# One attention pipeline for the first two blocks, weights queued later, the later casts moved from GpSimd to ScalarE, and the query permutation moved from the gate multiply to the exponential

## The chip, the cores and the metric

The kernel runs on one core of one Trainium2 chip. The metric is the device time of one execution in microseconds (us). Most executions of one kernel agree closely, but some run some per cent longer at a lower mean clock of TensorE. The runs therefore carry a state, "fast" or "slow".

In the text PE is TensorE, DVE is VectorE, ACT is ScalarE, POOL is GpSimd, and SP is the engine that issues most DMAs. "Clock" is the share of full speed that the throttle granted PE.

## The reference, cut to what matters

```python
# q, k, v: (4, 8, 768, 64); mem_k, mem_v: (4, 8, 8, 64)
for c in range(nc):                       # chunks of 32 queries
    k_ctx = k[:, :, l_start:r_end]        # 16 keys to the left, 8 to the right
    k_full = concatenate([mem_k, k_ctx]); v_full = concatenate([mem_v, v_ctx])
    a = softmax(q_c @ k_full.T / 8)
    out[:, :, c_start:c_end] = a @ v_full
x = out.transpose(0, 2, 1, 3).reshape(3072, 512)
return (relu(x @ w_gate) * (x @ w_val)) @ w_out     # FFN, 512 -> 1536 -> 512
```

The 3072 tokens are eight blocks of 384. Each block has four attention steps of 96 queries against 120 keys and 8 memory keys, then 12 FFN pieces (one for each 128 of the 1536 hidden columns) and three output products. An FFN piece is four matmuls with `w_gate` and four with `w_val`.

## The kernel before

The parts that the change and the argument touch, with cuts marked `...`. `dv`, `pl` and `act.copy` (`ac`) are copies on DVE, POOL and ACT. `x` is the output of the attention and `xT` its transpose; to "turn" a tile is to transpose it. `keep(n)` issues n matmuls whose results are never used, `outp` is one output product, and `u` counts the FFN pieces and products of a block. Keys and queries are loaded with three consecutive tokens to a partition, so after the transpose the queries of a step lie in the order "remainder by 3 first" (`t c`). The natural order is `c t`.

```python
def cast3(eng, c, n, a0=0, na=HP):        # fp32 -> f16, keys or queries of block n
    ...
def cast_v(eng, n):                       # values; memory rows by a second cast on POOL
    eng(vb_t[n % 2][:, :, :, 0:D], vraw[:, n % 2])
    ...
    pl(vb_t[n % 2][0:NMEM, :, :, 0:D], m4)
def turn_k(n): ...                        # transposing DMA on SP; turn_q(n) likewise
def diag(n): ...                          # DVE: transposed queries into a block-diagonal tile
def bands(n, eng): ...                    # copies of the transposed keys into four bands

class Step:
    def scores(self): ...                 # PE
    def soft(self):                       # ACT; the queries stay in the order t c
        ...
        act.activation(e.rearrange("p (h b) c -> p b h c" if self.early else "p (b h) c -> p b h c", b=2),
                       PS[:, 0:2, 0:384].rearrange("p b (h c) -> p b h c", h=4), ACT.Exp, scale=SCALE)
    def mask(self): ...                   # DVE: e = e * mask, both in SBUF
    def values(self): ...                 # PE
    def norm(self): ...                   # DVE: x_big
    def turn_dma(self): ...               # xT by a transposing DMA; turn_pe by PE and a copy

def dff(n, m, c0=0, c1=MB):               # an FFN piece
    ...                                   # PE, then ACT relu, then PE
    o, i0, i1 = gvT[n][:, m, c0:c1], vl_ps, g_relu[:, 0:w]
    if n not in EARLY:                    # blocks 2 to 7: the permutation is undone here
        o = o.rearrange("p (j c t) -> p j t c", t=R3, c=PP)
        i0, i1 = (z.rearrange("p (j t c) -> p j t c", t=R3, c=PP) for z in (i0, i1))
    dve.tensor_tensor(out=o, in0=i0, in1=i1, op=ALU.mult)

# between the FFN of blocks 0, 1 and the rest
cast3(dv, "k", 2)
...
turn_k(2)
cast3(dv, "q", 2)
turn_q(2)
...
outp(0, 0)
outp(0, 1)
cast_v(pl, 2)
diag(2)
bands(2, dv)
outp(0, 2)
...                                       # attention of block 2 among the products of block 1

for n in range(2, NBLK):                  # FFN of block n, attention of block n + 1, casts of n + 2
    for u in range(NDC + NT):
        ...
                if u == (10 if n == 2 else 7):
                    cast3(pl, "k", n + 2)
                    ...
                    cast3(pl, "q", n + 2)
                if u == vu[3]:
                    turn_k(n + 2)
                    turn_q(n + 2)
                if u == vu[3]:
                    cast_v(pl, n + 2)
```

The softmax here doesn't subtract the row's maximum and nothing guards it: scores larger than these inputs give would overflow.

## Time and profile before

Three runs gave 285.18, 288.53 and 282.09 us (288.53 is 2.3% above the fastest, so it counts as slow). The profiled run was a slow one (291.95 us, span 290.2, clock 0.952), so its stages are somewhat longer than those of a fast run.

The first cut is at block 1's first FFN piece, the others are where the output products of a block begin. This is the busy time by stretch. The columns are the stretch and its length, the busy time of PE, PEld (weight loads), DVE, ACT and POOL with the count of instructions, the PE clock, the DMA share and GB/s.

```profile
0.00:48.40 48.40, 38.42 (x297) 20.73 (x298) 23.07 (x60) 22.24 (x37) 36.75 (x77) 0.95 1.00 199
48.40:77.10 28.70, 28.70 (x161) 16.49 (x161) 10.60 (x19) 9.80 (x20) 4.45 (x5) 0.90 0.37 91
77.10:136.50 59.40, 43.96 (x305) 25.73 (x304) 28.79 (x57) 16.79 (x34) 10.38 (x7) 0.89 0.65 146
136.50:255.40 118.90, 107.96 (x732) 60.67 (x730) 69.31 (x108) 42.74 (x77) 42.12 (x43) 0.99 0.60 135
255.40:290.20 34.80, 31.27 (x172) 16.30 (x168) 11.24 (x16) 9.21 (x18) 0.00 (x0) 0.99 0.14 49
```

| stage | what runs in it |
|---|---|
| 0 to 48.4 ("front") | attention of blocks 0 and 1, four FFN pieces |
| 48.4 to 77.1 | the other 20 FFN pieces of blocks 0 and 1; PE never idle, but at clock 0.90 |
| 77.1 to 136.5 ("middle") | six output products, attention of blocks 2 and 3, FFN of block 2 |
| 136.5 to 255.4 ("four blocks") | products of block n, FFN of n + 1, attention of n + 2; four times |
| 255.4 to 290.2 ("tail") | what is left, with no attention |

The middle loses most: PE is busy 43.96 of 59.40 us there, and runs at clock 0.89 besides. The timeline shows why (start, duration, engine, line, operation; in brackets the engine's idle time just before it and what ended it).

```profile
77.83 0.95 DVE L169 CAST kn<-kraw 128x1536 f16<-128x1536 f32 x1
...
85.41 1.12 DVE L195 COPY qd<-qT 64x1536 f16<-64x1536 f16 x2 [5.44 <-DMA qT<-qn]
...
88.39 0.82 PE L242 MATMUL PS<-qd,kb 128*128 128x192 f16 x4 [3.38 <-DVE kb L221]
...
97.78 1.88 POOL L179 CAST vb<-memv 8x2048 f16<-8x2048 f32 x1
...
98.08 1.99 DVE L257 TENSOR_TENSOR ex<-ex,mask_int_t 128x768 f16<-128x768 f16 x1 [3.88 <-ACT ex L250]
...
100.13 0.43 PE L261 MATMUL PS<-vb,ex 128*128 128x66 f16 x8 [2.61 <-DVE ex L257]
```

Block 2's key cast starts at 77.83, after the last FFN piece. PE gets the bands at 88.39, 10.6 us later, having waited 3.38 us. At 98.08 a mask multiply beside a POOL cast takes 1.99 us, and the values product waits 2.61 us for it.

The groups of instructions (count, busy time and mean ns; then idle time before them, by releaser) give the cost of one operation.

```profile
L304 DVE TENSOR_TENSOR gvT<-PS,g_relu 128x384 f16<-128x384 f32 x92 | 67.7, 739 | 92.8 <-PE PS L298 91.3
...
L250 ACT ACTIVATE ex<-PS 128x768 f16<-128x768 f32 x32 | 26.0, 813 | 40.6 <-PE PS L242 29.3 <-DVE rinv L267 7.3 <-PE PS L238 4.0
L257 DVE TENSOR_TENSOR ex<-ex,mask_int_t 128x768 f16<-128x768 f16 x18 | 15.0, 833 | 7.5 <-ACT ex L250 7.5
```

### The profile page before, as it was taken

Reading aid. Unit: us, or ns where it says so; the run is one execution under the profiler, and the core shown is the slowest. Engines: PE = TensorE matmul, PEld = TensorE weight load, DVE = VectorE, ACT = ScalarE, POOL = GpSimd, SP = SyncE. Lnnn points to the kernel's source line nnn. Section 1 sums busy time; section 2 is a strip of 40 time slices with the busy share of each in tenths; the row PEclk is TensorE's granted clock in tenths of the full one; section 3 lists DMA queues with packets and bytes.
Section 4 is the critical chain, followed back from the end, with each engine's and each line's share of the span. In section 5 each row is a group of like instructions: output and inputs, shape, how many; then the busy total and the mean of one; then the engine's idle time right before and its main releaser. Section 6 shows DMA issues by size and latency. Waiting matters only on the chain.

```text
span 290.2 us, 4432 instructions
## 1 busy us (share of the span) xinstructions
PE 250.3 (86%) x1656; PEld 139.9 (48%) x1656; DVE 143.0 (49%) x258; ACT 100.8 (35%) x185; POOL 93.7 (32%) x131
## 2 busy tenths in 40 slices
PE   6697996999976488399977799889988999999995
PEld 2335553565523257155444455545555556645652
DVE  3418453344523316738355751875187517733630
ACT  2435564233221234134132423343334325423321
POOL 6828897022004500500454502652255140000000
PEclk9999797799997979969997999999999999999999
DMA  7998993930099519805399219971996180121002
GB/s 212 314 235 110 206 204 52 273 78 0 2 204 264 192 35 222 179 0 98 101 236 266 42 27 187 285 132 29 213 289 114 27 220 0 27 66 72 1 4 107
DMA packets 81237, 38.66 MB, mean 133 GB/s; under 512 B 53952, under 2 KB 78272, under 8 KB 81216
## 3 DMA queue, kind: packets, MB, share of 16 engines
q1 hardware_dynamic: 74208, 32.74, 48.0%
q0 software_dynamic: 5808, 4.72, 10.5%
q10 hardware_dynamic: 1200, 0.92, 1.0%
q8 instruction: 13, 0.21, 0.3%
q14 instruction: 8, 0.07, 0.1%
HBM read 29.72 MB, written 6.29 MB: 124 GB/s over the span
## 4 chain that ended last, share of the span: by engine, by line
PE 65%; DVE 19%; DMA 6%; POOL 3%; issue 2%; ACT 2%; SPq 1%; DVEq 0%; POOLq 0%; ACTq 0%
PE PS L293 18%; PE PS L298 18%; PE PS L313 16%; DVE ex L257 6%; DVE gvT L304 5%; PE PS L261 3%; PE PS L242 3%; DMA kT<-kn 3%; PE PS L356 2%; DVE x_big L270 2%; POOL kb L211 2%; DVE kb L211 2%; DMA kraw<-in_k_dram 1%; DMA qT<-qn 1%; PE PS L333 1%
## 5 line engine op out<-in xcount | busy, mean ns | idle before, releaser
L304 DVE TENSOR_TENSOR gvT<-PS,g_relu 128x384 f16<-128x384 f32 (+1 forms) x100 | 71.4, 718 | 94.8 <-PE PS L298 91.3
L293 PE MATMUL PS<-xT,w_gate_sb 128*128 128x384 f16 (+1 forms) x400 | 82.9, 332 | 1.1 <-ACT xT L280 1.1
L298 PE MATMUL PS<-xT,w_val_sb 128*128 128x384 f16 (+1 forms) x400 | 82.8, 332 | 0.0
L296 ACT ACTIVATE g_relu<-PS 128x384 f16<-128x384 f32 (+1 forms) x100 | 47.7, 477 | 60.0 <-PE PS L293 43.9
L313 PE MATMUL PS<-w_out_sb,gvT 128*128 128x512 f16 x288 | 66.5, 389 | 0.0
L298 PEld LDWEIGHTS <-w_val_sb 128*128 128x128 f16 x400 | 40.0, 101 | 26.3 <-issue 4.1
L293 PEld LDWEIGHTS <-w_gate_sb 128*128 128x128 f16 x400 | 39.7, 101 | 24.9 <-issue 4.8
L313 PEld LDWEIGHTS <-gvT 128*128 128x128 f16 x288 | 28.6, 100 | 33.6 <-issue 3.3
L250 ACT ACTIVATE ex<-PS 128x768 f16<-128x768 f32 x32 | 26.0, 813 | 40.6 <-PE PS L242 29.3
L323 ACT COPY o_sb<-PS 128x512 f32<-128x512 f32 x23 | 13.5, 587 | 56.6 <-PE PS L313 50.3
L176 POOL CAST vb<-vraw 128x2048 f16<-128x2048 f32 x6 | 11.4, 1894 | 41.7 <-DMA vraw<-in_v_dram 41.7
L261 PE MATMUL PS<-vb,ex 128*128 128x66 f16 x256 | 13.6, 195 | 11.5 <-DVE ex L257 10.0
L211 POOL COPY kb<-kT 128x480 f16<-128x480 f16 (+1 forms) x12 | 9.5, 889 | 42.2 <-DMA kT<-kn 42.2
L270 DVE TENSOR_TENSOR x_big<-PS,rinv 96x512 f16<-96x512 f32 x32 | 22.0, 686 | 1.1
L242 PE MATMUL PS<-qd,kb 128*128 128x192 f16 x96 | 13.2, 265 | 10.8 <-DVE kb L221 8.2
L169 POOL CAST kn<-kraw 128x1536 f16<-128x1536 f32 x5 | 7.3, 1469 | 44.4 <-DMA kraw<-in_k_dram 44.4
L261 PEld LDWEIGHTS <-ex 128*128 128x128 f16 x256 | 10.9, 99 | 20.7 <-ACT g_relu L296 8.4
L257 DVE TENSOR_TENSOR ex<-ex,mask_int_t 128x768 f16<-128x768 f16 x18 | 15.0, 833 | 7.5 <-ACT ex L250 7.5
L242 PEld LDWEIGHTS <-kb 128*128 128x128 f16 x96 | 7.8, 104 | 12.9 <-DVE kb L221 9.1
L169 POOL CAST qn<-qraw 128x1536 f16<-128x1536 f32 (+1 forms) x8 | 10.7, 1336 | 9.5 <-DMA qraw<-in_q_dram 9.5
L179 POOL CAST vb<-memv 8x2048 f16<-8x2048 f32 x6 | 12.1, 2023 | 0.4
L195 DVE COPY qd<-qT 64x1536 f16<-64x1536 f16 x12 | 7.7, 645 | 6.8 <-DMA qT<-qn 6.7
(106 smaller groups left out, 152.1 us busy)
## 6 DMA issues: line engine op xcount, KB each, us to landing
out_dram<-o_sb SPq DMA_DIRECT2D x23, 256.0 KB, 2.3
vraw<-in_v_dram SPq DMA_DIRECT2D x24, 240.0 KB, 7.2
kraw<-in_k_dram SPq DMA_DIRECT2D x7, 768.0 KB, 7.8
qraw<-in_q_dram SPq DMA_DIRECT2D x7, 768.0 KB, 8.7
vraw<-in_v_dram SPq DMA_DIRECT2D x2, 768.0 KB, 13.7
w_out_sb<-in_moe_w_out_dram POOLq DMA_DIRECT2D x3, 512.0 KB, 15.3
w_gate_sb<-in_moe_w_gate_dram POOLq DMA_DIRECT2D x2, 512.0 KB, 7.6
w_val_sb<-in_moe_w_val_dram POOLq DMA_DIRECT2D x2, 512.0 KB, 9.4
```

Of the source, the lines that this page charges most:

```text
L169: eng(d.rearrange("p a t (x d) -> p a x t d", x=2), raw[c][:, i, 2 * a0:2 * a0 + 2 * na].rearrange("p (a x) t d -> p a x t d", x=2))
L211: eng(dst(1, c0 + r, [[128, nj], [R3, 40]]), src(kT, TS * t + P + (r > 0), [[PP, nj], [1, 40]]))
L242: pe.matmul(o.rearrange("p (x t c) -> p x t c", x=2, t=R3), lhsT=self.kb[:, a, j, :], rhs=qd_t[i][:, a].rearrange("p x (t c) -> p x t c", ...
L250: act.activation(e.rearrange("p (h b) c -> p b h c" if self.early else "p (b h) c -> p b h c", b=2), PS[:, 0:2, 0:384].rearrange("p b (h c ...
L257: dve.tensor_tensor(out=e, in0=e, in1=m8, op=ALU.mult)
L261: pe.matmul(PS[:, 2 + h // 4, VW * (h % 4):VW * (h % 4) + VW], lhsT=self.ex[:, h, :], rhs=self.vb[:, self.j, h, :], start=True, stop=True)
L270: dve.tensor_tensor(out=self.x.rearrange("p (b h d) -> p b h d", b=2, h=4), in0=o[:, :, :, 0:D], in1=rb, op=ALU.mult)
L293: pe.matmul(g_ps, lhsT=w_gate_sb[:, f, 128 * m:128 * m + 128], rhs=xTs[n][:, f, c0:c1], start=(f == 0), stop=(f == NFC - 1))
L296: act.activation(g_relu[:, 0:w], g_ps, ACT.Relu)
L298: pe.matmul(vl_ps, lhsT=w_val_sb[:, f, 128 * m:128 * m + 128], rhs=xTs[n][:, f, c0:c1], start=(f == 0), stop=(f == NFC - 1))
L304: dve.tensor_tensor(out=o, in0=i0, in1=i1, op=ALU.mult)
L313: pe.matmul(PS[:, o], lhsT=gvT[n][:, m, 128 * t:128 * t + 128], rhs=w_out_sb[:, m, :], start=(m == 0), stop=(m == NDC - 1))
```

## The change

Its intent: (1) start the attention of block 1 directly behind that of block 0, as one pipeline of eight steps, with x of a step turned two steps behind its scores; (2) let the first weights queue on POOL behind block 1's key casts; (3) make the casts of the later blocks earlier and on ACT (values on DVE), with the memory rows brought by DMA in place of a POOL cast; (4) undo the permutation of the queries in the exponential and not in the gate multiply, so that x and everything after it is in natural order. The diff, cut to its core (left out: the scores of blocks 2 to 7 now lie in PSUM with gaps, 96 of every 128 columns; block 2's FFN is no longer cut in halves; x of block 2 is turned by DMA and no longer by PE; the loads are split otherwise):

```diff
 def soft(self):
-    act.activation(e.rearrange("p (h b) c -> p b h c" if self.early else "p (b h) c -> p b h c", b=2),
-                   PS[:, 0:2, 0:384].rearrange("p b (h c) -> p b h c", h=4), ACT.Exp, scale=SCALE)
+    if self.early:
+        ...                                      # as before
+    else:
+        s_ps = PS[:, 0:2].rearrange("p b (h c) -> p (b h) c", h=4)[:, :, 0:QB]
+        act.activation(e.rearrange("p h (c t) -> p h t c", t=R3),
+                       s_ps.rearrange("p h (t c) -> p h t c", t=R3), ACT.Exp, scale=SCALE)
 ... dff():
-    if n not in EARLY:
-        o = o.rearrange("p (j c t) -> p j t c", t=R3, c=PP)
-        i0, i1 = (z.rearrange("p (j t c) -> p j t c", t=R3, c=PP) for z in (i0, i1))
-    dve.tensor_tensor(out=o, in0=i0, in1=i1, op=ALU.mult)
+    dve.tensor_tensor(out=gvT[n][:, m, c0:c1], in0=vl_ps, in1=g_relu[:, 0:w], op=ALU.mult)
 ... front (steps of block 0, FFN pieces, steps of block 1, written out, become:)
+    def pipe(s, mid=(), end=()):
+        ...                                      # scores, exp, mask of step s; values of s - 1
+        if s >= 2:
+            st[s - 2].turn_pe(act.copy if s % 2 else dv)
+    pipe(0, [lambda: keep(3)])
+    ...
+    cast3(pl, "k", 1, 0, 2)
+    cast3(pl, "k", 1, 2, 2)
+    load_w(0, 256)                               # was ahead of step 0
+    pipe(1)
+    ...
 ... among the FFN pieces of blocks 0 and 1:
+                    if (n, m) == (1, 7):
+                        cast3(ac, "k", 2, 0, 2)
+                    ...
+                    if (n, m) == (0, 10):
+                        cast3(ac, "q", 2, 2, 2)
+                        turn_q(2)
+                    ...
+                    if (n, m) == (1, 10):
+                        diag(2)
+                    if (n, m) == (1, 11):
+                        bands(2, dv)
 ... middle: steps of block 2 between all six products, casts of block 3 on ACT:
+    outp(1, 1)
+    turn_k(3)
+    v_part(st[3])                                # its xT by a transposing DMA, behind turn_k(3)
+    cast3(ac, "q", 3, 0, 2)
+    outp(1, 2)
+    cast3(ac, "q", 3, 2, 2)
+    turn_q(3)
 ... loop:
-                    cast3(pl, "k", n + 2)
-                    cast3(pl, "q", n + 2)
-                    cast_v(pl, n + 2)
+                if u == 0:
+                    diag(n + 1)                  # was u == 1
+                if u == 1:
+                    bands(n + 1, pl)
+                if u == 3:
+                    cast_v(dv, n + 1, 0, 2)
+                ...
+                if u in (7, 9):
+                    cast3(ac, "k", n + 2, u - 7, 2)
+                if u == 12:
+                    turn_k(n + 2)
+                    cast3(ac, "q", n + 2, 0, 2)
+                if u == 13:
+                    cast3(ac, "q", n + 2, 2, 2)
+                    turn_q(n + 2)
```

## The prediction

> **What bounds it now.** The profile is of a slow run (span 290.2 us; timed median 285.2). TensorE (PE) is busy 86% and 65% of the chain of waits, so PE idle and half-clock time can be won. By stage (busy time by stretch):
>
> - 0 to 48.4 us: attention of blocks 0, 1 with 4 FFN pieces;
> - 48.4 to 77.1: the other 20 FFN pieces, PE never idle, clock 0.90;
> - 77.1 to 139.9: six output products, attention of blocks 2, 3, 12 FFN pieces; PE busy 47.1 of 62.8, clock 0.86 to 0.91. A piece is 1.30 us at full clock, a product 2.6; 15.6 + 15.6 + two attentions of 3.5 (26.9 of the cleanest block less 15.6 and 7.8) is 38, so 24 are lost;
> - four blocks: 31.1, 29.0, 28.6, 26.9 (the last has no POOL casts);
> - the tail, 34.5, near PE's own time.
>
> Two losses. (1) Late operands: PE waits 3.4 us for block 2's key copies (casts start at 77.8, after all FFN pieces; then a 4.3 us transpose and DVE copies), 4.9 for block 3's, 2.5 for block 4's. Each gap is followed by 3.5 to 6 us at clock about 0.5. The Trainium skill, "TensorE: Matmul & The Clock Gate", Part 1, has an idle window of about 3.4 us halve the clock; here 2.5 us gaps sufficed. (2) The mask multiply takes 0.53 us alone, up to 1.99 beside POOL casts (timeline at 98.1, 137.6). The skill, "SBUF — State Buffer", "Who interferes with whom", says a DVE multiply with both inputs in SBUF contends with GpSimd's reads; the trace agrees.
>
> **What changes.**
> - Block 2's casts go to ACT among the FFN pieces (0.85 us per half, from ACT's 768-element cast), so transposes are nearly done when the output products begin. ACT was 35% busy.
> - POOL loses key, query and value casts (1.5, 1.5, 1.9 us) and the memory-row cast (2.0) per block; value casts go to DVE (estimate 0.63 per half, from 0.95 for 1536 elements). Band copies stay on POOL.
> - The gate multiply loses its permutation: 0.80 to 0.56 us, as blocks 0, 1 show.
> - Front: one pipeline, no FFN pieces before step 6; first scores about 1.5 us earlier (14.2 now). Warm steps about 2 us; I expect some 2 us of wait at block 1's band copies.
> - Weights start some 5 us later, but move as fast (205 GB/s written) and the DMA hole at 24 to 27 goes; landed by about 42 to 46, before use.
>
> **Sum (estimates).** Front 48.4 to 43. FFN pieces 28.7 to 26 (no half clock). Middle 62.8 to 42: 38 plus 4 of new waits (block 2's query transpose and band copies; xT by DMA queued behind block 3's key transpose). Four blocks 115.6 to 108. 290.2 - 5.4 - 2.7 - 21 - 7.6 = 253.5 span; reported time ran 1.75 above, so 255 us. Nearly all is PE idle or half-clock time, so critical.
>
> **What would show it.** PE busy over 93% and full clock from 45 us on; mask multiply near 0.55 but at a few places (band copies); gate multiply 0.56; no PE wait over 2 us after 45; block 1's first FFN piece near 43; blocks 26.5 to 27.5 apart.
>
> **What would make it wrong.** Weights landing late; 3 us waits at block 1's band copies or before block 2's FFN, with half clock after; DVE blocked by the diagonal copy at each block's start (query transpose late), 1 us a block; more half-clock time in the front.
>
> Predicted 255 us, 80% range 246 to 266; faster by over 2%: 0.96, within 2%: 0.03, slower: 0.01.

## More of the kernel before

The exponential takes 813 ns. The Trainium skill, "ScalarE: Activation LUTs", section "What ACT_TABLE_LOAD costs", gives 186 ns plus 0.833 ns per element for such an instruction, from which 826 ns is the estimate for 768 elements, so the trace agrees. The mask multiply takes 833 ns on average, but the median is 537: of the 24 of blocks 2 to 7 only eight take over 1 us.

## The result, and the profile after

| | runs (us) | median | ratio of fast runs, 95% interval |
|---|---|---|---|
| before | 285.18, 288.53 (slow), 282.09, 282.45 | 283.81 | |
| after | 262.10, 264.72 (slow), 260.74, 260.35 | 261.42 | 0.921 (0.913 to 0.929) |

A ratio here is the mean time of one kernel's fast runs over that of the other's of the same rounds, so it is not quite the ratio of the medians. (A fifth run of after is 260.23 us; it is not in the median.) The change makes the kernel some 8% faster. 261.4 is inside the predicted range, and 6.4 us above the predicted 255.

The profiled run of after was a fast one (262.10 us, span 260.4, clock 0.985), while that of before was slow, so a part of the differences between the two traces is the state. The busy time by stretch, at the same cuts:

```profile
0.00:40.20 40.20, 33.21 (x299) 18.43 (x300) 24.99 (x63) 20.54 (x33) 27.97 (x56) 0.96 1.08 219
40.20:66.20 26.00, 25.95 (x160) 15.65 (x160) 11.03 (x20) 12.61 (x24) 0.78 (x2) 1.00 0.85 191
66.20:110.00 43.80, 38.89 (x267) 21.21 (x265) 22.83 (x48) 24.59 (x33) 4.07 (x9) 0.96 0.76 176
110.00:224.90 114.90, 106.04 (x725) 59.88 (x722) 57.20 (x113) 61.48 (x90) 16.48 (x29) 1.00 0.61 141
224.90:260.40 35.50, 31.28 (x173) 16.30 (x169) 8.04 (x16) 9.19 (x18) 0.00 (x0) 0.99 0.14 48
```

| stage | before | after | change |
|---|---|---|---|
| front | 48.4 | 40.2 | -8.2 |
| 20 FFN pieces | 28.7 | 26.0 | -2.7 |
| middle | 59.4 | 43.8 | -15.6 |
| four blocks | 118.9 | 114.9 | -4.0 |
| tail | 34.8 | 35.5 | +0.7 |

Most of the gain is in the front and the middle. The four blocks gave 4.0 us where the prediction had 7.6, although POOL's work there fell from 42.12 to 16.48 us. ACT's rose from 42.74 to 61.48, and PE still idles 114.90 - 106.04 = 8.9 us, at full clock. The groups say what became longer:

```profile
L300 DVE TENSOR_TENSOR gvT<-PS,g_relu 128x384 f16<-128x384 f32 x96 | 53.0, 556 | 96.3 <-PE PS L298 75.0 <-ACT g_relu L296 21.1
...
L250 ACT ACTIVATE ex<-PS 128x768 f16<-128x768 f32 x24 | 35.2, 1468 | 20.3 <-PE PS L237 20.2
L257 DVE TENSOR_TENSOR ex<-ex,mask_int 128x768 f16<-128x768 f16 x24 | 14.1, 586 | 7.3 <-ACT ex L246 3.9 <-ACT ex L250 3.3
L261 PE MATMUL PS<-vb,ex 128*128 128x66 f16 x256 | 13.6, 195 | 9.9 <-DVE ex L257 8.7 <-DVE vb L172 0.7 <-DVE x_big L270 0.5
```

The gate multiply fell to 556 ns, and the mask multiply to 586, both as predicted. (586 contains the steps of the front, with one of 1.23 us; from block 2 on every mask multiply takes about 0.55 us.) The exponential rose from 813 to 1468 ns. Gate multiplies now wait 21.1 us in all for ACT's relu, which does not show in their line of before, and the values product (L261) waits 8.7 us for masks. One step of a block shows the chain:

```profile
160.44 1.47 ACT L250 ACTIVATE ex<-PS 128x768 f16<-128x768 f32 x1 [0.61 <-PE PS L237]
...
161.69 0.53 ACT L296 ACTIVATE g_relu<-PS 128x384 f16<-128x384 f32 x1
...
162.26 0.56 DVE L300 TENSOR_TENSOR gvT<-PS,g_relu 128x384 f16<-128x384 f32 x1 [1.22 <-ACT g_relu L296]
...
162.73 0.55 DVE L257 TENSOR_TENSOR ex<-ex,mask_int 128x768 f16<-128x768 f16 x1
...
163.43 0.42 PE L261 MATMUL PS<-vb,ex 128*128 128x66 f16 x8 [0.42 <-DVE ex L257]
```

In this trace ACT and DVE take their instructions in the order of the program. The relu of the next FFN piece stands behind the long exponential (it starts at 161.69, where the exponential ends at 160.44 + 1.47 = 161.91). The gate multiply waits 1.22 us for the relu, and the mask stands behind the gate multiply. PE then idles 0.42 us. In the middle and at a block's start two other waits are left:

```profile
85.24 1.52 SPq L274 DMA_TRANSPOSE xT<-x_big  x1
...
88.00 0.81 PE L293 MATMUL PS<-xT,w_gate_sb 128*128 128x384 f16 x4 [2.18 <-issue]
...
149.64 1.44 DVE L188 COPY qd<-qT 64x1536 f16<-64x1536 f16 x2 [0.80 <-DMA qT<-qn]
...
151.72 0.81 PE L298 MATMUL PS<-xT,w_val_sb 128*128 128x384 f16 x4 [0.29 <-DVE gvT L300]
```

The last xT of block 2 is issued behind block 3's key transpose, and PE idles 2.18 us before block 2's FFN. (The profile books it as "issue", that is, it names no releaser; that the transpose is the cause is tested by e4 below.) The diagonal copy at a block's start waits 0.80 us for the query transpose, and the gate multiplies stand behind it.

### The profile page after: what moved, and what is told of

The parts are those of the page before. It is cut to its first block, busy times and chain, and to the rows that moved or that the text cites. A ratio compares the mean times of both kernels' runs of the same rounds, so it can differ in the third digit from the quotient of the medians.

```text
span 260.4 us, 4350 instructions
## 1 busy us (share of the span) xinstructions
PE 235.4 (90%) x1611; PEld 131.5 (50%) x1611; DVE 124.1 (48%) x257; ACT 128.4 (49%) x197; POOL 49.3 (19%) x96
## 4 chain that ended last, share of the span: by engine, by line
PE 56%; DVE 16%; issue 8%; DMA 7%; ACT 6%; SPq 3%; POOL 0%; ACTq 0%; DVEq 0%; POOLq 0%
PE PS L309 19%; PE PS L298 14%; PE PS L293 13%; DVE gvT L300 5%; DVE ex L257 5%; PE PS L261 4%; ACT g_relu L296 4%; DMA qT<-qn 3%; DVE x_big L270 3%; DMA vraw<-in_mem_v_dram 2%; PE PS L352 2%; DMA vx<-in_v_dram 2%; PE PS L237 2%; SPq L141 2%; DVE qd L188 1%
## 5 line engine op out<-in xcount | busy, mean ns | idle before, releaser
L300 DVE TENSOR_TENSOR gvT<-PS,g_relu 128x384 f16<-128x384 f32 x96 | 53.0, 556 | 96.3 <-PE PS L298 75.0
L293 PE MATMUL PS<-xT,w_gate_sb 128*128 128x384 f16 x384 | 78.7, 328 | 2.7 <-issue 2.2
L298 PE MATMUL PS<-xT,w_val_sb 128*128 128x384 f16 x384 | 79.1, 329 | 2.1 <-DVE gvT L300 1.9
L296 ACT ACTIVATE g_relu<-PS 128x384 f16<-128x384 f32 x96 | 47.8, 498 | 43.4 <-PE PS L293 22.4
L250 ACT ACTIVATE ex<-PS 128x768 f16<-128x768 f32 x24 | 35.2, 1468 | 20.3 <-PE PS L237 20.2
L204 POOL COPY kb<-kT 128x320 f16<-128x320 f16 (+1 forms) x15 | 11.0, 830 | 130.2 <-DMA kT<-kn 130.2
L261 PE MATMUL PS<-vb,ex 128*128 128x66 f16 x256 | 13.6, 195 | 9.9 <-DVE ex L257 8.7
L261 PEld LDWEIGHTS <-ex 128*128 128x128 f16 x256 | 11.1, 99 | 20.4 <-ACT g_relu L296 15.6
L257 DVE TENSOR_TENSOR ex<-ex,mask_int 128x768 f16<-128x768 f16 x24 | 14.1, 586 | 7.3 <-ACT ex L246 3.9
L165 ACT CAST qn<-qraw 128x768 f16<-128x768 f32 x12 | 10.0, 836 | 0.0
L165 ACT CAST kn<-kraw 128x768 f16<-128x768 f32 x12 | 9.9, 827 | 0.0
L352 PE MATMUL PS<-v,step 128*120 128x512 f16 x27 | 8.8, 450 | 0.0
```

What stands on the lines that cost most here:

```text
L165: eng(d.rearrange("p a t (x d) -> p a x t d", x=2), raw[c][:, i, 2 * a0:2 * a0 + 2 * na].rearrange("p (a x) t d -> p a x t d", x=2))
L250: act.activation(e.rearrange("p h (c t) -> p h t c", t=R3), s_ps.rearrange("p h (t c) -> p h t c", t=R3), ACT.Exp, scale=SCALE)
L257: dve.tensor_tensor(out=e, in0=e, in1=m8, op=ALU.mult)
L261: pe.matmul(PS[:, 2 + h // 4, VW * (h % 4):VW * (h % 4) + VW], lhsT=self.ex[:, h, :], rhs=self.vb[:, self.j, h, :], start=True, stop=True)
L293: pe.matmul(g_ps, lhsT=w_gate_sb[:, f, 128 * m:128 * m + 128], rhs=xTs[n][:, f, c0:c1], start=(f == 0), stop=(f == NFC - 1))
L296: act.activation(g_relu[:, 0:w], g_ps, ACT.Relu)
```

## The experiments

Theory A says that the strided f16 write of the exponential, through ACT's order, is what the prediction left out. Its rivals, with the letters that the expectations use: B, the casts that were put on ACT and DVE made the blocks long; C, the exponential is long because it now reads scores with gaps in PSUM; D, the diagonal copy (and what it waits for) costs the blocks; E, the xT of block 2 by DMA costs the middle. A second group asks what each named part of the change is worth, and a third what remains. The three groups ran on three chips. The kernel before ran in each group, but in the first group only one of its seven runs was fast (280.66 us), so there is no interval there, and those four are compared by their own fast runs and by stages. A difference in the total can contain one of chips; the stages are the safer measure. All kernels gave correct results.

### e1_contig: the exponential writes side by side

```diff
-  act.activation(e.rearrange("p h (c t) -> p h t c", t=R3),
-                 s_ps.rearrange("p h (t c) -> p h t c", t=R3), ACT.Exp, scale=SCALE)
+  act.activation(e.rearrange("p h (c t) -> p h c t", t=R3),
+                 s_ps.rearrange("p h (t c) -> p h c t", t=R3), ACT.Exp, scale=SCALE)
```

The same elements go to the same places; only the order of the walk differs. The write is now contiguous and the read from PSUM steps by 32 elements, three at a time. The gaps in PSUM stay.

> Only the order in which the exponential of blocks 2 to 7 walks its elements changes: it writes ex contiguously and reads the scores strided, instead of reading contiguously and writing every third f16. Theory A (the strided write makes the exponential 1.47 us instead of 0.81; relu, gate multiply and mask behind it come late and the values product waits 0.42 us at each of four steps a block): exponential 0.81 to 0.85 us, blocks about 27 us apart instead of 28.7, time about 254 to 256 us (after: 261.4). Rival B (the blocks are long because of the casts put on ACT and DVE): the exponential shortens but blocks stay above 28.2 and the time above 259. Rival C (the exponential is long because the scores now lie with gaps in PSUM, 96 of 128): it stays near 1.47 us and the time at 261.

Measured: 249.90 and 249.90 us fast, 256.89 and 256.27 slow. The fast runs are 10 to 12 us below those of after, and better than the 254 to 256 expected. The profiled run was a slow one, with half clock at 24 to 37 us; its only other stretch of half clock before the tail, at 92 to 96 behind a wait of 2.51 us, has its like in after (89 to 93 behind 2.18 us), so the later stages can be compared. The groups:

```profile
L250 ACT ACTIVATE ex<-PS 128x768 f16<-128x768 f32 x24 | 19.5, 811 | 12.8 <-PE PS L237 12.7
...
L261 PE MATMUL PS<-vb,ex 128*128 128x66 f16 x256 | 14.0, 198 | 0.0
```

The timeline of the same step:

```profile
159.63 0.81 ACT L250 ACTIVATE ex<-PS 128x768 f16<-128x768 f32 x1 [0.16 <-PE PS L237]
...
160.34 0.48 ACT L296 ACTIVATE g_relu<-PS 128x384 f16<-128x384 f32 x1
...
161.00 0.56 DVE L300 TENSOR_TENSOR gvT<-PS,g_relu 128x384 f16<-128x384 f32 x1 [0.63 <-PE PS L298]
...
161.47 0.55 DVE L257 TENSOR_TENSOR ex<-ex,mask_int 128x768 f16<-128x768 f16 x1
...
162.17 0.42 PE L261 MATMUL PS<-vb,ex 128*128 128x66 f16 x8
```

The exponential is back at 811 ns, the gate multiply waits for PE and no longer for the relu, and PE waits for no mask at all (0.0 against 9.9 us). A block takes 26.92 us in place of 28.73 (mean distance of the starts of the products of blocks 2 to 6). Middle and four blocks together take 148.9 us in place of 158.7. Theory A stands: this one order of a walk costs some 10 us. Rival C falls, since the gaps stayed and the exponential is short, and B falls too, since the casts stayed on ACT and DVE.

### e2_pool_casts: the later key and query casts back on POOL

```diff
-  cast3(ac, "k", n + 2, u - 7, 2)
+  cast3(pl, "k", n + 2, u - 7, 2)      # likewise both query casts
```

> The key and query casts inside the main loop go back from ACT to POOL; the exponential stays strided. Rival B (ACT casts stretch the blocks): blocks drop towards 27 us, time 255 to 257. Theory A: the values product still waits for the exponential at every step; POOL casts contend with the mask multiply again (up to 1.2 to 2 us in some steps); blocks 28.7 to 29.5, time 261 to 265.

Measured: 264.27, 262.03, 264.21 and 263.99 us, all fast, against 260.2 to 262.1 of after. A block takes 28.97 us against 28.73. Relieving ACT of all these casts while the exponential stays long does not shorten a block. What the casts cost on POOL (0.3 us a block with the short exponential, e9 below) is too little to hide the 1.8 us of e1. Rival B falls here as well.

### e3_diag_u1: the diagonal copy one FFN piece later

```diff
-  if u == 0:
-      diag(n + 1)
   if u == 1:
+      diag(n + 1)
       bands(n + 1, pl)
```

> The diagonal copy of the next block's queries is issued one FFN piece later in the main loop (behind the second gate multiply instead of the first). Theory D (DVE stands at the diagonal copy until the query transpose lands, so the second gate multiply is late and the fourth FFN piece waits 0.3 to 0.9 us for its PSUM bank): that wait disappears in all five blocks, about 2 to 3 us in sum, time 258.5 to 260. If the wait only moves to the next piece: 261 to 262.

Measured: 257.85, 260.10 and 257.87 us fast, 262.20 slow. The copy's wait for the query transpose fell from 4.8 us to nothing, and a block takes 28.03 us, 0.7 less. Rival D is true, but small: some 2.5 us, a quarter of what e1 gave.

### e4_turn_pe: the last xT of block 2 by PE and not by DMA

```diff
-  v_part(st[3])
+  st[3].values(); st[3].norm()
   cast3(ac, "q", 3, 0, 2)
   outp(1, 2)
+  st[3].turn_pe(dv)
```

> Block 2's last x is turned by PE behind the last output product instead of by DMA behind block 3's key transpose. Theory E (the DMA turn stands behind the key transpose in the SP queue and PE idles 2.2 us before block 2's FFN, then runs 3.5 to 4.5 us at half clock): idle falls to about 1 us, no half clock at 88 to 92, gain 1.2 (idle) + about 2 (clock), time 257.5 to 260. If the half clock stays although the gap is 1 us: gain 1, time about 260.5.

Measured: 262.03, 261.84, 261.22 and 264.16 us, all fast: no gain, where 257.5 to 260.5 was expected. The timeline:

```profile
86.01 0.81 PE L293 MATMUL PS<-xT,w_gate_sb 128*128 128x384 f16 x4 [0.45 <-DVE xT L280]
...
91.43 1.12 DVE L188 COPY qd<-qT 64x1536 f16<-64x1536 f16 x2 [3.29 <-DMA qT<-qn]
...
93.20 1.44 PE L298 MATMUL PS<-xT,w_val_sb 128*128 128x384 f16 x4 [2.47 <-DVE gvT L300]
```

The wait before block 2's FFN is gone (0.45 us; it starts at 86.01 and not at 88.00). So rival E has the cause of this wait right. But the query transpose of block 3 landed hardly earlier (the diagonal copy behind it starts at 91.43, in after at 91.72), so DVE stood 3.29 us at that copy, and PE 2.47 behind it; 1.44 us for four matmuls (0.65 at full clock) shows half clock after it. The gap moved and was not removed: the middle needs the casts and transposes of block 3 earlier as well.

### e5_weights_first: the first weights ahead of block 1's key casts

```diff
+  load_w(0, 256)
   pl(vx16, vx)
+  load_w(256, 256)
   cast_v3(dv, 0, 4, 4)
   ...                                  # both removed from their places behind the casts
```

> The first two pairs of weight loads are issued before block 1's key casts again, as in the kernel before; the rest is as after. If the order matters as intended (weights then share the DMA queues with block 1's k, q, v from about 10 us on): block 1's key cast starts at 15.5 to 17 us instead of 14.0, its band copies end 1.5 to 3 us later than 23.4, first FFN piece of block 1 at 42 to 43.5 us instead of 40.2, time 263 to 265. If the DMA has room: cast within 0.5 us of 14.0, time 260.5 to 262, and this part of the change was worth nothing.

Measured: 264.82, 265.85 and 264.24 us fast, 269.38 slow; ratio to before 0.934 (0.929 to 0.939), against 0.921 of the change. By the quotient 0.934/0.921 = 1.014, the order of the queue is worth about 3.7 us; the two intervals just overlap, so the size is not sure. In this profile (a slow run) block 1's key cast starts at 16.91 us and not at 13.97, and the first output product at 74.63, against 70.78 in the slow run of e1, whose front is that of after.

### e6_turn_1_behind: x turned one step behind the scores

```diff
-  if s >= 2:
-      st[s - 2].turn_pe(act.copy if s % 2 else dv)
+  if 1 <= s <= 2 * NJ:
+      st[s - 1].turn_pe(act.copy if s % 2 else dv)
```

> In the pipeline of 8 steps x is turned one step behind the scores instead of two, so PE stands at each turn until the reciprocal and the multiply of the same step are done (0.2 + 0.69 us plus signals, 1.0 us in the kernel before). If that is what two steps of distance bought: 0.6 to 1 us more PE wait at each of 8 steps, first FFN piece of block 1 at 44 to 48 us instead of 40.2, time 265 to 269. If DVE, which is over 90% busy at 16 to 23 us, bounds the steps anyway: first piece within 1.5 us of 40.2 and time 261 to 263.

Measured: 264.56, 267.33 and 264.13 us fast, 269.67 slow; ratio 0.936 (0.925 to 0.946), so about 4 us slower than the change, though these intervals overlap too. The first output product starts at 69.5 us, against 66.25 in after and 64.8 to 67.1 in e2, e3 and e4, whose front is the same (all fast runs).

### e7_late_casts: block 2's casts, transposes and bands after the FFN pieces again

```diff
   # removed from among the FFN pieces; after them:
+  cast3(dv, "k", 2); cast_kx(dv, 1); turn_k(2)
+  cast3(dv, "q", 2); turn_q(2)
+  ...
+  outp(0, 0); outp(0, 1); diag(2); bands(2, dv); outp(0, 2)
+  ...                                  # steps of block 2 among the products of block 1
```

> Block 2's casts are back behind the FFN pieces of blocks 0 and 1 and on DVE, and its diagonal and band copies behind the second output product, as before the change; front and main loop stay as after. If the early casts on ACT are the main gain of the middle stretch: PE idles about 4 us before block 2's scores and up to 5 us before its FFN, each with half clock after; the stretch from the first output product to block 2's outputs grows by 8 to 12 us and the time is 269 to 274. If the gain of that stretch came from elsewhere (no half pieces, DMA turns, no POOL casts): below 265.

Measured: 278.11, 275.14 and 275.88 us fast, 279.41 slow; ratio 0.971 (0.967 to 0.976), some 14 us slower than the change, and more than the 269 to 274 us expected. The middle takes 56.9 us in place of 43.8. Two of its waits:

```profile
80.48 0.82 PE L237 MATMUL PS<-qd,kb 128*128 128x192 f16 x4 [3.43 <-DVE kb L216]
...
104.24 1.44 PE L293 MATMUL PS<-xT,w_gate_sb 128*128 128x384 f16 x4 [3.41 <-DMA xT<-x_big]
```

The 3.4 us wait of before at block 2's scores is back, with half clock at 80 to 83 us; the wait for xT by DMA before block 2's FFN grew from 2.18 to 3.41. Two waits for masks, of 3.33 and 2.19 us, came besides. Making these operands early is the largest part of the change that was tested. The edit also puts the casts on DVE and shifts the steps of block 2 by two products, so the 14 us belong to the whole arrangement.

### e8_all: e1 and e3, and block 3's casts one product earlier

```diff
   # e1 and e3, and in the middle:
   outp(0, 2)
+  cast3(ac, "k", 3, 0, 2)              # both key casts ahead of outp(1, 0)
   ...
   outp(1, 0)
+  turn_k(3)                            # was after outp(1, 1)
   ...
   outp(1, 1)
+  turn_q(3)                            # was after outp(1, 2)
+  st[3].values(); st[3].norm()
   outp(1, 2)
+  st[3].turn_pe(dv)                    # as in e4
```

> Contiguous exponential, diagonal copy one piece later, block 3's key and query casts and transposes one output product earlier, block 2's last x turned by PE behind the last product. If moving the query transpose was what the PE turn alone lacked (there the 2.2 us wait came back as 2.5 us at block 3's diagonal copy): no PE wait above 1 us and no half clock from 45 to 100 us, blocks 26.5 us apart, time 246 to 250 in its fast runs (slow ones, with half clock at 24 to 37 us, some 6 more). If not: about 250 to 252, as the contiguous exponential alone less 2.

Measured: 247.48 and 245.92 us fast, 251.69 and 251.30 slow; ratio to before 0.870 (0.863 to 0.877). The middle takes 37.7 us with PE busy 37.1, and the four blocks 105.0 with PE busy throughout. What e4 could not win alone is won together with the earlier casts and transposes. (e8 holds several edits at once; e1 alone has a middle of 41.2 us, and the share of each of the others is not measured.)

### e9_contig_pool: e1, with key, query and value casts on POOL

```diff
-  cast3(ac, "k", n + 2, u - 7, 2)
+  cast3(pl, "k", n + 2, u - 7, 2)      # query casts and both value casts likewise; with e1's write
```

> Contiguous exponential as before in that experiment (blocks 26.9 us apart, fast runs 249.9), but the key, query and value casts of the main loop go to POOL. If the prediction was right that POOL casts beside the mask multiply cost the old blocks their time: several mask multiplies at 1.2 us or more, blocks 27.8 to 28.8, fast runs 253 to 257. If the casts' place is worth nothing: blocks within 0.2 us of 26.9, fast runs about 250.

This asks what taking these three casts off POOL was worth, once the exponential is short. It doesn't bring back the memory-row cast of 2.0 us a block, beside which the mask multiply of 1.99 us ran, nor the old places of the casts. Measured: 256.96 and 255.01 us fast, 259.10 and 258.92 slow; ratio to before 0.901 (0.892 to 0.910). A block takes 27.23 us against 26.92 of e1, so 0.3 us is what these casts cost a block on POOL. Mask multiplies of up to 1.2 us are back among the blocks, where e1 has none over 0.56. The fast runs are 5 to 7 us above those of e1. The two did not run on the same chip; by the traces the four blocks give 1.2 us of that (108.9 against 107.7) and the middle 1.1 (42.4 against 41.2). Where the rest lies is open.

### e10_all_keep: e8 and eight idle matmuls in front of step 4

```diff
+  keep(8)                              # results never used
   pipe(4)
```

> The combined kernel plus eight idle matmuls (about 1.7 us at full clock) in front of block 1's first scores, where PE waits some 2 us for the band copies. If that gap is what drops the clock in the front (half clock from about 24 to 28 us in its fast runs, to 37 in the slow ones of others): no half clock after 24 us, fast runs 244 to 246, and the spread between fast and slow runs (245.9 to 251.7) mostly goes. If other gaps of the front suffice: no change, 246 to 251.

PE waits there for block 1's bands, 1.99 us in after and 1.57 in e8, and after it the clock is halved. The busy time by stretch of after, of e8, and of this kernel:

```profile
24.00:26.00 2.00, 2.00 (x6) 1.05 (x6) 0.56 (x1) 0.75 (x1) 2.00 (x3) 0.50 0.80 98
```

```profile
24.00:26.00 2.00, 2.00 (x13) 1.00 (x10) 0.56 (x1) 0.81 (x1) 2.00 (x4) 0.58 0.90 93
```

```profile
24.00:26.00 2.00, 2.00 (x17) 0.94 (x16) 0.57 (x3) 0.81 (x1) 2.00 (x3) 1.00 0.91 66
```

The clock is 1.00, and not 0.50 or 0.58, and 17 matmuls ran in place of 6 or 13. Measured: 245.78, 244.76, 245.69, 245.57 and 245.14 us fast, 248.46 slow; median 245.63, ratio to before 0.864 (0.859 to 0.869). Against e8 the fastest time fell only from 245.9 to 244.8, but five of six runs stay within 1.1 us. The middle and the four blocks:

```profile
65.60:103.30 37.70, 37.08 (x270) 20.95 (x268) 22.87 (x49) 19.67 (x33) 4.16 (x9) 1.00 0.86 201
103.30:208.40 105.10, 105.10 (x727) 59.97 (x724) 56.76 (x113) 51.95 (x90) 15.95 (x29) 1.00 0.66 154
```

This version beats both kernels.

### e11_keep_act_bands: four of block 1's eight band copies on ACT

```diff
   else:
       e = kT_t[0]
+      eng = act.copy if n in EARLY else eng
```

> As the one before, and four of block 1's eight band copies on ACT instead of DVE. If DVE (over 95% busy at 16 to 23 us) sets the wait at block 1's bands: its first scores 0.6 to 1.2 us earlier, time 0.5 to 1.5 us less than the one before. If ACT is late itself (query copies until 22.3): no gain.

Measured: 245.73, 244.90, 246.13, 244.73 and 245.72 us fast, 248.97 slow; ratio 0.864 (0.858 to 0.869). It is the same as e10: the scores of step 4 start at 24.19 us and not at 24.44, a quarter of a microsecond, and the total shows none of it.

### e12_probe: the exponential by itself

Eight exponentials of e1's shape were put at the end of e1, with results never used, and with other steps of the write.

```diff
+  act.activation(o(kn, 1), s_ps, ACT.Exp, scale=SCALE)      # L609; L610 to L612 with steps 2, 3, 4
+  act.activation(o(vraw, 1), s_ps, ACT.Exp, scale=SCALE)    # L613, fp32; L614 with step 3
+  act.activation(o(kn, 1) in the change's order, ...)       # L615
+  act.activation(o(kn, 1) in e1's order, ...)               # L616: strided read, contiguous write
```

> The contiguous-exponential kernel with eight more exponentials of 128x768 at its end, which write nothing that is used: f16 results side by side, every 2nd, 3rd, 4th element, fp32 side by side and every 3rd, then the change's own order and the repaired one. If a gap between written elements doubles the cost: about 0.81 us for the side-by-side ones and the repaired order, about 1.47 for every 2nd to 4th and for the change's order. If only steps beyond some distance cost: every 2nd stays at 0.81. If short runs of 32 elements cost, not the step: every 3rd stays at 0.81 and the change's order takes 1.47.

One run, 262.56 us, state unknown; only the durations are used. The groups, in the order of their busy time:

```profile
L612 ACT ACTIVATE kn<-PS 128x768 f16<-128x768 f32 x1 | 1.9, 1867 | 0.0
...
L611 ACT ACTIVATE kn<-PS 128x768 f16<-128x768 f32 x1 | 1.4, 1444 | 0.1
L615 ACT ACTIVATE kn<-PS 128x768 f16<-128x768 f32 x1 | 1.4, 1426 | 0.0
...
L614 ACT ACTIVATE vraw<-PS 128x768 f32<-128x768 f32 x1 | 1.2, 1179 | 0.0
...
L610 ACT ACTIVATE kn<-PS 128x768 f16<-128x768 f32 x1 | 1.0, 1021 | 0.0
...
L613 ACT ACTIVATE vraw<-PS 128x768 f32<-128x768 f32 x1 | 0.9, 896 | 0.0
...
L609 ACT ACTIVATE kn<-PS 128x768 f16<-128x768 f32 x1 | 0.8, 811 | 0.9 <-DVE o_sb L315 0.9
...
L616 ACT ACTIVATE kn<-PS 128x768 f16<-128x768 f32 x1 | 0.8, 811 | 0.0
```

The expectations did not hold as stated. Side by side the f16 write takes 811 ns; with every second, third and fourth element 1021, 1444 and 1867. From step 2 on each further element of the step adds 423 ns. An fp32 write pays too, but less (896 to 1179 at step 3). The strided read from PSUM costs nothing: L616 reads with a step and writes side by side in 811 ns. So the dear part is shown to be the write. Why it grows so is not settled here.

## Why the prediction was right or wrong

Predicted 255 us (246 to 266), faster by over 2%; measured 261.4. Two errors of size partly cancelled: the front came out 2.8 us better, and middle and blocks 8.7 us worse. Point by point:

- **The term that failed: "Four blocks 115.6 to 108", and with it the sign "blocks 26.5 to 27.5 apart".** They were 28.7 apart. The prediction put the middle and the four blocks, in its own cuts, at 42 + 108 = 150 us; they took 43.8 + 114.9 = 158.7. It saw the permutation leave the gate multiply and booked that gain. It didn't ask where the permutation went, and booked nothing for an exponential that now writes every third element. That cost measured 1468 - 813 = 655 ns on each of 24 exponentials, and 8.7 us of PE waiting for masks. With only this write repaired (e1), middle and four blocks take 41.2 + 107.7 = 148.9 us, about the predicted 150. So the cost that was left out explains this part of the miss, and the experiment shows it.
- **The reason given for the blocks, POOL's casts, is only partly borne out.** That POOL's casts slow the mask multiply is true, and the Trainium skill, "SBUF — State Buffer", section "Who interferes with whom", says why a DVE multiply with both inputs in SBUF meets GpSimd's reads. The trace agrees: 833 ns on average and up to 1.99 us before, 586 ns after. But the part that was tested is worth little: with the key, query and value casts back on POOL and the write repaired (e9) a block is only 0.3 us longer. What the memory-row cast cost the old blocks was not tested. (The fast runs differ by more, 5 to 7 us over two chips, and that is not explained.)
- **Middle "62.8 to 42".** The mechanism was right: the early casts, with what follows from them, are worth some 14 us (e7). The named new wait, xT "queued behind block 3's key transpose", came (2.18 us at 88.0). The sign "no PE wait over 2 us after 45" failed by that one. e4 showed that removing this wait alone gains nothing, and e8 one set of edits that does gain.
- **"DVE blocked by the diagonal copy at each block's start".** The prediction named it as a risk of 1 us a block. e3 measured 0.7.
- **Front "48.4 to 43".** It was 40.2, so 2.8 us better than predicted. The sign "block 1's first FFN piece near 43" came at 40.25. The two named parts of it, weights later (e5, about 3.7 us) and x two steps behind (e6, about 4 us), both point the way predicted, with sizes that are not sure. The first scores came at 10.99 us in place of 14.16, 3.2 us earlier where 1.5 was predicted. The 2 us wait at block 1's bands came as predicted (1.99 us), and half clock followed (0.50 at 24 to 26 us).
- **FFN pieces "28.7 to 26".** 26.0: exact. The weights were in time, for PE was busy 25.95 of the 26.00 us.
- **"PE busy over 93% and full clock from 45 us on".** From 45 to 256 us PE was busy 197.4 of 211.2 us, 93.5%, at clock 0.99. Full clock failed at one place, 89 to 93 us, behind the wait of 2.18 us.
- **Half clock after short gaps.** The Trainium skill, "TensorE: Matmul & The Clock Gate", Part 1, has an idle window of about 3.4 us halve the clock, and lets that window run freely. Gaps were shorter: a wait of 1.99 us at 23.5 us in after, and one of 2.18 at 88.0, were followed by clock 0.50. But the length of a wait did not decide it: behind the same wait before block 2's FFN the clock stayed at 1.00 in e5 (2.20 us, up to 96.39) and in e6 (2.21 us, up to 91.25), while in e4 two waits of 1.26 and 1.45 us, the second up to 23.66, were followed by 0.50 at 25 to 28 us. So half clock can follow such shorter waits and need not; what decides is not shown here.

The sum closes: front -2.8, middle and four blocks +8.7, tail +1.0 (35.5 against 34.5), the FFN pieces 0, are 6.9 us in the span, 260.4 against the predicted 253.5.

## What to carry to other kernels

When a change takes a permutation out of one instruction, find the instruction that has it now, and cost its reads and writes apart: here a strided read was free and a strided f16 write nearly doubled the instruction. An engine that is far from full can still be the one that the others wait for, when a long instruction stands ahead of a short one that they need: ACT was 54% busy in the blocks (61.48 of 114.90 us), and its long instruction delayed PE three instructions later. Where a wait is removed and nothing is won, look for the next operand that comes late at the same place, and move both. And do not count on a short wait being harmless to the clock: time it where it matters.

## What the Trainium skill lacked or had wrong

- "ScalarE: Activation LUTs" gives the time of an ACTIVATE by its element count and the kind of its operands, and its rate agrees for a write side by side (811 ns here for 768 elements, 826 estimated from the page). It lacks the step of the write: f16 with every second, third and fourth element took 1021, 1444 and 1867 ns, fp32 with every third 1179 against 896.
- "SBUF — State Buffer", section "Door 1: The DMA port swizzle", has a note that strides of up to 8 bf16 or 4 fp32 elements are free. For ACT's writes f16, two bytes as bf16 is, was already 210 ns longer with a step of 2. fp32 with a step of 3 was 283 ns longer, which the note's other condition, two hits or more in a line of 16 bytes, may cover. The same note says that any access to PSUM that isn't contiguous slows matmuls down; of ACT it says nothing, and ACT's strided read of PSUM cost nothing here (811 ns both ways).
- "TensorE: Matmul & The Clock Gate", Part 1, has about 3.4 us of idleness halve the clock; of shorter idles it says that they can make the clock swing, but gives no length. Here waits of 1.99, 2.18 and 2.47 us (after, e4) were followed by clock 0.50, and two of 2.20 and 2.21 us were not (e5, e6). With eight idle matmuls in such a gap (e10) it stayed at 1.00.
- "SBUF — State Buffer", section "Who interferes with whom", gives the rule for a DVE multiply with two SBUF inputs but no time for it: in before, 0.53 us alone became up to 1.99 us beside a POOL cast.
